# Softmax sums, layernorm centring, weight decoding and instruction order changed in a capped-attention and spatial-gating kernel

## The chip, the cores and the metric

The kernel runs on one core of a Trainium2 chip (trn2). The metric is device time in microseconds of one execution, lower is better. TensorE (PE) multiplies matrices, VectorE (DVE), ScalarE (ACT) and GpSimd (POOL) work on elements, and SyncE (SP) issues almost all DMAs.

## The reference

Capped attention over 4 batches, 12 heads, 448 positions, head width 64, followed by a gated block with a spatial product; all in float32.

```
scores = cap * tanh((q @ k^T / 8) / cap)             # per head
attn   = exp(scores - max) / (sum + 1e-9)
x      = concat over heads of attn @ v                # 4 x 448 x 768
h      = gelu_tanh(x @ w_in)                          # 768 -> 1024
u, v   = h[:, :512], h[:, 512:]
v_n    = (v - mean) / sqrt(var + 1e-6) * g_ln         # over 512
v_s    = w_sg @ v_n + b_sg                            # over positions
out    = x + (u * v_s) @ w_out                        # 512 -> 768
```

## The kernel before, in words

Heads go in pairs, 6 pairs per batch; two pairs make a group, so there are 12 groups, numbered g = 3*batch + group. The 448 keys of a pair are three chunks of 128 and a tail of 64; the tails of a group's two pairs share one step. A step of a group is: scores of a key chunk on TensorE into a PSUM tile `sc` (lines 513 to 547), tanh and exp on ScalarE into a tile `p` of 128 x 896 (591, 593), and the product with the values on TensorE (549 to 568). Most products are made of three float32r matmuls over a high and a low part; the parts are made by a copy and a subtraction (`cop` and `sub`, lines 321 to 326) or, for queries and keys, by a scaling and a fused multiply-subtract (502, 509).

The softmax denominators are sums of `p` over keys. Which engine adds the chunks is chosen for each group in SUMS (line 29). Mode 0: each of the 7 tiles `p` goes to TensorE, which sums over the partitions with a matmul by ones into `den` (line 451). Mode 1: VectorE adds chunks 2 and 3 to chunk 1 for both pairs (line 604, four adds), and the tail tile still goes to TensorE by itself, so 3 units are left. Mode 2: VectorE also adds the halves of the tail tile (two further adds on 64 partitions), and 2 units are left. Two units share a step on TensorE, `den_op`; the last of a batch may be alone.

The denominators are copied out, spread through DRAM, inverted and loaded back (`recip`, 626). Then `gated(b)` (650) runs for each batch: `norm` (666) scales x and splits it, `hv(t)` (719) makes the v half for each block of 128 positions with gelu, statistics, power on GpSimd and layernorm, `hu(f)` (758) the u half, `vsg(f)` (773) the spatial product with bias and gate, `outp(c)` (795) the output product, residual and store. The weights arrive as 64-bit floats and are decoded to a high and a low part by `decode` (359): low, high, shift and sign bits, a whole-number addition on GpSimd (396), then a copy and a subtraction.

Every operation is recorded by `plan.op` (169) with the engines on which it can run and a cost. The order in which they are issued, and the engine of each, is written out by hand: ORDER (37) lists the number of each operation times two, plus one for its second engine. `run` (201) issues them so; each engine then works through its own instructions in that order, and DMAs wait in SP's queue in that order too. Operations wait only for data and for tiles of small pools: 5 `p` tiles (SIZES, 23), 2 `sc` tiles, 3 raw query/key tiles.

Of the kernel before, what the change touches and what calls it, by code (L numbers as in the profile page):

```python
# [28 lines left out]
SUMS = (0, 1, 1, 1, 0, 1, 1, 1, 2, 2, 2, 2)  # L29
PLAIN = (1, 0, 0, 1, 0, 0, 0, 0, 0, 0, 0, 0, 1, 0, 0, 0, 0, 0, 0, 0, 0, 0, 0, 0)  # L30
RETIRE = (10, 10, 12, 11, 0, 0)
# [186 lines left out]
def kernel(  # L218
# [30 lines left out]
    def tiles(n, shape, dtype, name):  # L249
        return [wp.tile(shape, dtype, name=f"{name}{i}") for i in range(n)]  # L250

    win = tiles(2, [128, KD, DFF], FP32R, "win")
    wout = tiles(2, [128, KF, DM], FP32R, "wout")
    wsg = tiles(2, [128, NC, S], FP32R, "wsg")
    LO = NP + 31
# [645 lines left out]
```

## Time and profile before

| | |
|---|---|
| median of 3 runs | 377.01 us (376.59 to 377.73) |
| the profiled execution's own time | 376.92 us |
| its span | 375.1 us |
| busy: PE / PEld / DVE / ACT / POOL | 370.3 / 251.9 / 301.3 / 211.3 / 40.0 us |
| instructions: PE / DVE / ACT / POOL | 2064 / 559 / 275 / 39 |
| DMA | 39.65 MB, 106 GB/s mean |

The span runs from the first to the last instruction or transfer; the execution's own time has 1.8 us around it. PE is the matmul itself, PEld the loading of weights beside it. A group of instructions is named by its line in the kernel and by its tiles, out<-in. A chain of waits is followed back from the last instruction to whatever released it. Instruction durations on VectorE and ScalarE overlap a little: the next one starts some 0.1 us before the one ahead of it has ended, so a sum of durations is more than the time that they fill.

### The profile page before, as it was taken

What the parts mean: (1) busy time and instruction counts of PE and PEld (TensorE: products, weight loads), DVE (VectorE), ACT (ScalarE), POOL (GpSimd) and SP (SyncE); (2) the same over time, 40 slices, a digit from 0 to 9 for tenths busy, and PEclk for the clock granted to TensorE, in tenths of its full rate; (3) what the DMA queues carried; (4) which work ended last, traced back from release to release, by engine and by line L of the source; (5) the groups of instructions that cost most, each with busy time, mean ns of one, the idle gap of its engine ahead of it and who ended that gap; (6) DMA issues with size and microseconds to landing.
All of it is one profiled execution on the core that took longest, in us unless ns stands there. A gap on an engine that the chain in (4) does not pass through costs nothing.

```text
span 375.1 us, 5508 instructions
## 1 busy us (share of the span) xinstructions
PE 370.3 (99%) x2064; PEld 251.9 (67%) x2064; DVE 301.3 (80%) x559; ACT 211.3 (56%) x275; POOL 40.0 (11%) x39
## 2 busy tenths in 40 slices
PE   9999999999999999999999999999999999999995
PEld 4334343455877497546478976486889999889995
DVE  2799999999999999989894779779276988438763
ACT  5999999995685758697914377751031411033200
POOL 0231121510310312030000100000001000001000
PEclk9999999999999999999999999999999999999999
DMA  7898264454371244146520022202120101400004
GB/s 262 290 285 280 91 187 151 118 158 150 98 255 44 65 135 172 43 134 201 150 80 2 20 73 46 76 3 78 36 74 24 47 5 50 171 2 0 2 0 171
DMA packets 23130, 39.65 MB, mean 106 GB/s; under 512 B 5472, under 2 KB 17728, under 8 KB 23104
## 3 DMA queue, kind: packets, MB, share of 16 engines
q1 hardware_dynamic: 22816, 38.96, 33.0%
q8 instruction: 16, 0.26, 0.3%
q10 hardware_dynamic: 288, 0.34, 0.3%
q14 instruction: 10, 0.08, 0.1%
HBM read 33.28 MB, written 6.02 MB: 105 GB/s over the span
## 4 chain that ended last, share of the span: by engine, by line
PE 96%; DVE 2%; ACT 1%; issue 0%; DVEq 0%; ACTq 0%
PE ps L552 15%; PE ps L725 13%; PE ps L763 13%; PE sc L520 11%; PE ps L800 10%; PE ps L780 9%; PE sc L800 6%; PE den L451 5%; PE sc L528 3%; PE sc L763 3%; PE ps L562 3%; PE sc L725 2%; PE sc L536 2%; PE sc L780 1%; PE ps L352 1%; DVE p L604 1%
## 5 line engine op out<-in xcount | busy, mean ns | idle before, releaser
L593 ACT ACTIVATE p<-p,cap 128x896 f32<-128x896 f32 x84 | 84.8, 1041 | 0.7
L591 ACT ACTIVATE p<-sc 128x896 f32<-128x896 f32 x63 | 56.4, 911 | 15.7 <-PE sc L520 6.9
L552 PE MATMUL ps<-p,v 128*64 128x448 f32 x288 | 61.3, 551 | 0.0
L604 DVE TENSOR_TENSOR p<-p,p 128x896 f32<-128x896 f32 (+1 forms) x48 | 53.8, 1130 | 5.5 <-PE ps L552 3.0
L725 PE MATMUL ps<-win,rg 128*128 128x512 f32 x205 | 50.3, 391 | 0.0
L763 PE MATMUL ps<-rg,win 128*128 128x448 f32 x223 | 50.3, 366 | 0.0
L520 PEld LDWEIGHTS sc<-hl 64*128 64x128 f32 x378 | 32.7, 184 | 25.6 <-ACT p L591 11.7
L520 PE MATMUL sc<-hl 64*128 64x448 f32 x378 | 48.3, 383 | 0.0
L763 PEld LDWEIGHTS ps<-rg,win 128*128 128x128 f32 x223 | 41.8, 188 | 4.4 <-issue 0.7
L725 PEld LDWEIGHTS ps<-win,rg 128*128 128x128 f32 x205 | 38.4, 188 | 8.3 <-issue 0.7
L396 POOL TENSOR_TENSOR stage<-stage 128x512 int32<-128x512 int32 (+1 forms) x20 | 30.6, 1532 | 113.4 <-DVE stage L391 58.1
L552 PEld LDWEIGHTS ps<-p,v 128*64 128x64 f32 x288 | 17.5, 136 | 34.1 <-issue 22.0
L706 ACT ACTIVATE t<-ps 128x448 f32<-128x448 f32 (+1 forms) x25 | 14.2, 567 | 46.4 <-PE ps L725 29.3
L800 PE MATMUL ps<-rg,wout 128*128 128x448 f32 x166 | 39.7, 368 | 0.0
L800 PEld LDWEIGHTS ps<-rg,wout 128*128 128x128 f32 x166 | 30.9, 188 | 5.3 <-issue 2.7
L780 PE MATMUL ps<-wsg,rg 128*128 128x448 f32 x130 | 30.6, 369 | 0.0
L711 ACT ACTIVATE t<-t 128x448 f32<-128x448 f32 (+1 forms) x30 | 18.0, 602 | 20.6 <-DVE t L708 20.6
L739 POOL TENSOR_TENSOR sm<-sm,pw 128x1 f32<-128x1 f32 x14 | 8.7, 627 | 186.7 <-DVE sm L737 177.9
L708 DVE SCALAR_TENSOR_TENSOR t<-t,ps 128x448 f32<-128x448 f32 (+1 forms) x25 | 16.2, 647 | 13.3 <-ACT t L706 13.3
L780 PEld LDWEIGHTS ps<-wsg,rg 128*128 128x128 f32 x130 | 24.0, 188 | 4.1 <-issue 1.0
L800 PE MATMUL sc<-rg,wout 128*128 128x448 f32 x98 | 24.3, 365 | 0.0
L591 ACT ACTIVATE p<-sc,qsc 128x896 f32<-128x896 f32 x21 | 21.0, 1005 | 5.4 <-PE sc L536 1.9
(115 smaller groups left out, 468.2 us busy)
## 6 DMA issues: line engine op xcount, KB each, us to landing
raw<-in_qk_dram SPq DMA_DIRECT2D x22, 448.0 KB
stage<-in_w_in_dram SPq DMA_DIRECT2D x12, 512.0 KB
n<-spread SPq DMA_DIRECT2D x24, 224.0 KB
out_dram<-x SPq DMA_DIRECT2D x23, 224.0 KB
v<-in_vp_dram SPq DMA_DIRECT2D x24, 192.0 KB
stage<-in_w_out_dram SPq DMA_DIRECT2D x8, 384.0 KB
u<-in_w_sgT_dram SPq DMA_DIRECT2D x4, 224.0 KB
vt<-in_vt_dram SPq DMA_DIRECT2D x12, 64.0 KB
```

Of the source, the lines that this page charges most:

```text
L396: nc.gpsimd.tensor_tensor(out=a.bitcast(I32), in0=a.bitcast(I32), in1=hi, op=ALU.add)
L451: nc.tensor.matmul(out=den.t[32 * j:32 * j + 32, :S], lhsT=ones_sb[:, kind, NP - 1 - kind - p:NP + 31 - kind - p], rhs=src.t[:, h, :], sta ...
L520: nc.tensor.matmul(out=sc.t[:, h, :S], lhsT=hl[s].t[rows, w, 1, 128 * c - 128:128 * c], rhs=hl[s].t[rows, m, 0], start=(k == 0), stop=(k = ...
L552: nc.tensor.matmul(out=pav[s].t[64 * h:64 * h + 64, :S], lhsT=v[s].t[:, 128 * (c - 1) + 64 * h:128 * (c - 1) + 64 * h + 64], rhs=p.t[:, h, ...
L591: op(name("tanh", s, c), "act", c_act(2 * S, True, raw_scores), lambda p=p, sc=sc, r=raw_scores: nc.scalar.activation(out=p.t, in_=sc.t[:, ...
L593: op(name("exp", s, c), "act", c_act(2 * S, False, True), lambda p=p: nc.scalar.activation(out=p.t, in_=p.t, func=ACTF.Exp, scale=cap_sb), ...
L604: op(name("add", s, t), "dve", c_tt(2 * S), lambda: nc.vector.tensor_tensor(out=a.t[rows], in0=a.t[rows], in1=p.t[rows], op=ALU.add), rd=[ ...
L711: op(tag + " tanh", "act", c_act(n), lambda: nc.scalar.activation(out=view(), in_=view(), func=ACTF.Tanh, scale=GELU_C * GELU_A), wr=[sq])
L725: nc.tensor.matmul(out=ps.t[:, :HF], lhsT=(xl if a else xh)[c].t[:, t * 128:t * 128 + 128], rhs=win[w][:, c, HF:], start=(c == 0 and k == ...
L763: nc.tensor.matmul(out=ps.t[:, :S], lhsT=win[w][:, c, f * 128:(f + 1) * 128], rhs=(xl if a else xh)[c].t[:, :S], start=(c == 0 and k == 0) ...
L780: nc.tensor.matmul(out=ps.t[:, :S], lhsT=(vl if a else vh)[c].t[:, f * 128:(f + 1) * 128], rhs=wsg[w][:, c, :], start=(c == 0 and k == 0), ...
L800: nc.tensor.matmul(out=ps.t[:, :S], lhsT=wout[w][:, f, c * 128:(c + 1) * 128], rhs=(gl if a else gh)[f].t[:, :S], start=(f == 0 and k == 0 ...
```

## The change

SUMS changes for groups 4 to 7, so that VectorE adds more chunks. A mode 3 is written but no group uses it. The "high" step of the decoding can run on ScalarE too. The layernorm is split otherwise: centring, `mean - v`, is one instruction on VectorE or ScalarE that needs only the mean; the multiplication by the inverse deviation goes into the making of the high and low parts, with the deviation as a scalar from a tile; since the sign is turned, the gain `g_ln` is negated once (`gneg`). The statistics tile `sm` is tracked in two parts. Small tiles are allocated between the weight tiles and constants after the pools. Six stores (batch 2, columns 5, and batch 3, columns 0 to 4) are issued as two halves of 112 KB. ORDER is a new table of 1587 entries (1574 before); its text is left out here.

```diff
-SUMS = (0, 1, 1, 1, 0, 1, 1, 1, 2, 2, 2, 2)
+SUMS = (0, 1, 1, 1, 1, 2, 2, 2, 2, 2, 2, 2)
+LANES = (17, 18, 19, 20, 21, 22)
...
-    win = tiles(2, [128, KD, DFF], FP32R, "win")
-    wout = tiles(2, [128, KF, DM], FP32R, "wout")
-    wsg = tiles(2, [128, NC, S], FP32R, "wsg")
+    win = tiles(1, [128, KD, DFF], FP32R, "winh")
+    gneg, cap_sb = small(KF, "gneg"), small(1, "cap")
+    win += tiles(1, [128, KD, DFF], FP32R, "winl")
...
+    op("gneg", "dve", 0.15, lambda: nc.vector.tensor_scalar(
+        out=gneg, in0=g_sb, scalar1=-1.0, scalar2=None, op0=ALU.mult), rd=[k_const], wr=[k_neg])
...
-        def high_bits():
+        def high_bits(e):
             _, hi, a = words()
-            nc.vector.tensor_scalar(out=a, in0=f32(hi), scalar1=2.0 ** -112, scalar2=None, op0=ALU.mult)
+            if e == "dve":
+                nc.vector.tensor_scalar(out=a, in0=f32(hi), scalar1=2.0 ** -112, scalar2=None, op0=ALU.mult)
+            else:
+                nc.scalar.activation(out=a, in_=f32(hi), func=ACTF.Copy, scale=2.0 ** -112)
...
-            op(name("layernorm", t), "dve", 0.55, lambda: nc.vector.tensor_scalar(
-                out=vv(), in0=vv(), scalar1=sm.t[:, 6:7], scalar2=sm.t[:, 0:1],
-                op0=ALU.subtract, op1=ALU.mult), rd=[sm], wr=[v2])
+            def center(e):
+                if e == "dve":
+                    nc.vector.tensor_scalar(
+                        out=vv(), in0=vv(), scalar1=sm.t[:, 6:7], scalar2=-1.0, op0=ALU.subtract, op1=ALU.mult)
+                else:
+                    nc.scalar.activation(out=vv(), in_=vv(), func=ACTF.Identity, scale=-1.0, bias=sm.t[:, 6:7])
+
+            def both(tag, rows, hi, lo, rd, wr_hi, wr_lo):
+                def high(e):
+                    if e == "dve":
+                        nc.vector.tensor_scalar(out=hi(), in0=v2.t[rows, :HF], scalar1=sm.t[rows, 0:1], scalar2=None, op0=ALU.mult)
+                    else:
+                        nc.scalar.activation(out=hi(), in_=v2.t[rows, :HF], func=ACTF.Copy, scale=sm.t[rows, 0:1])
...
+                op("%d v%s lo %d" % (b, *tag), "dve", c_tt(HF) + 0.06, lambda: nc.vector.scalar_tensor_tensor(
+                    out=lo(), in0=v2.t[rows, :HF], scalar=sm.t[rows, 0:1], in1=f32(hi()), op0=ALU.mult, op1=ALU.subtract),
+                   rd=rd + [(sm, "r"), wr_hi], wr=[wr_lo], fast=True)
...
-                cop(name("v hi", t), lambda: h.t, vv, HF, [v2], [h])
-                sub(name("v lo", t), lambda: lo.t, vv, lambda: f32(h.t), HF, [v2, h], [lo])
+                both(("", t), slice(0, 128), lambda: h.t, lambda: lo.t, [v2], (h, 0), (lo, 0))
...
-                out=tt.t[:, :S], in0=ps.t[:, :S], scalar=g_sb[:, f:f + 1], in1=bsg_sb, op0=ALU.mult, op1=ALU.add),
-               rd=[ps, k_const, k_bsg], wr=[tt])
+                out=tt.t[:, :S], in0=ps.t[:, :S], scalar=gneg[:, f:f + 1], in1=bsg_sb, op0=ALU.mult, op1=ALU.add),
+               rd=[ps, k_neg, k_bsg], wr=[tt])
...
+                parts = 2 if not last and b * KD + c in LANES else 1
+                for m in range(parts):
+                    sm = slice(sl.start + cols * m // parts, sl.start + cols * (m + 1) // parts)
+                    op(name("store", c) + "abc"[n + m + (parts > 1)], eng, ISSUE, lambda sl=sm, queue=queue: queue.dma_start(
+                        out=outT[b, c][:, sl], in_=x.t[:, sl]), rd=[(x, sl.start)], size=128 * cols // parts * 4)
```

Read through the codes of both tables, the new one gives TensorE 17 `den_op` steps instead of 21, VectorE 58 adds instead of 48, and ScalarE 9 of the 20 "high" steps, 8 of the 14 centrings and 5 of the 21 scalings of queries and keys, none of which it had; VectorE takes over ScalarE's three denominator copies, the four high copies of the spatial weights, and four x and two g copies, and gives away two evacuations of x, two high copies of `win` and one tail copy.

## Rows read from the trace of the kernel before

**Rows 1.** The page: busy time (share), granted clock in 40 slices, the chain's shares.
```profile
PE 370.3 (99%) x2064; PEld 251.9 (67%) x2064; DVE 301.3 (80%) x559; ACT 211.3 (56%) x275; POOL 40.0 (11%) x39
...
PEclk9999999999999999999999999999999999999999
...
PE 96%; DVE 2%; ACT 1%; issue 0%; DVEq 0%; ACTq 0%
```

**Rows 2.** The chain that ended last, in order: start us, us, what.
```profile
53.45 2.12 DVE p L604
...
63.45 1.64 PE den L451 x16
...
70.37 0.89 PE den L451 x8
...
269.84 5.45 PE ps L725 x24
...
363.32 1.22 PE sc L800 x6
```

**Rows 3.** Stretches: us, busy us of each engine (instructions), clock, DMA, GB/s.
```profile
12.50:50.00 37.50, 37.50 (x262) 14.49 (x262) 35.13 (x58) 36.66 (x42) 8.18 (x5) 1.00 0.65 209
50.00:87.50 37.50, 37.44 (x254) 16.42 (x247) 36.27 (x56) 34.93 (x41) 9.08 (x5) 1.00 0.56 173
87.50:125.00 37.50, 37.50 (x194) 28.00 (x194) 35.80 (x84) 23.95 (x38) 6.44 (x6) 1.00 0.39 120
125.00:162.50 37.50, 37.50 (x230) 23.47 (x228) 35.82 (x68) 28.26 (x38) 8.20 (x7) 1.00 0.38 115
```

**Rows 4.** Line 604, the adds: duration min/median/max, first and last start.
```profile
L604 DVE TENSOR_TENSOR p<-p,p x48: 1076/1084/2209, 26.3 to 255.8; 128x896 f32<-128x896 f32 x40, 64x896 f32<-64x896 f32 x8
```

**Rows 5.** Groups of instructions: xcount | busy us, mean ns | idle before, releasers.
```profile
L593 ACT ACTIVATE p<-p,cap 128x896 f32<-128x896 f32 x84 | 84.8, 1041 | 0.7
...
L591 ACT ACTIVATE p<-sc 128x896 f32<-128x896 f32 x63 | 56.4, 911 | 15.7 <-PE sc L520 6.9 <-DVE p L604 6.6 <-PE ps L552 1.1
L604 DVE TENSOR_TENSOR p<-p,p 128x896 f32<-128x896 f32 (+1 forms) x48 | 53.8, 1130 | 5.5 <-PE ps L552 3.0 <-ACT p L593 1.9
...
L509 DVE SCALAR_TENSOR_TENSOR hl<-raw,root,hl 128x832 fp32r<-128x832 f32 x21 | 22.6, 1077 | 0.1
...
L502 DVE TENSOR_SCALAR hl<-raw,root 128x832 fp32r<-128x832 f32 x21 | 14.4, 686 | 3.2 <-DMA raw<-in_qk_dram 2.3 <-PE sc L520 0.8
...
L382 DVE TENSOR_SCALAR stage<-stage 128x512 f32<-128x512 f32 (+1 forms) x20 | 7.7, 391 | 2.9 <-DMA stage<-in_w_in_dram 2.9
...
L741 DVE TENSOR_SCALAR t<-t,sm 128x512 f32<-128x512 f32 x14 | 7.7, 555 | 2.2 <-POOL sm L739 2.1
...
L297 DVE CAST rg<-u 128x448 fp32r<-128x448 f32 x9 | 3.5, 388 | 0.1
...
L299 ACT ACTIVATE wsg<-u 128x448 fp32r<-128x448 f32 x4 | 2.3, 572 | 0.0
...
L297 DVE COPY t<-den 128x448 f32<-128x448 f32 x1 | 0.6, 623 | 0.3 <-PE den L451 0.3
```

**Rows 6.** In order of time, the start and the end: start us, us, instruction.
```profile
1.17 1.28 ACT L341 ACT_TABLE_LOAD   x1 [1.17 <-PEq L887]
...
6.51 0.65 DVE L502 TENSOR_SCALAR hl<-raw,root 128x832 fp32r<-128x832 f32 x1 [2.33 <-DMA raw<-in_qk_dram]
...
10.26 0.76 DVE L382 TENSOR_SCALAR stage<-stage 128x512 f32<-128x512 f32 x2 [1.64 <-DMA stage<-in_w_in_dram]
...
371.27 0.69 DVE L810 SCALAR_TENSOR_TENSOR x<-sc,x 128x224 f32<-128x224 f32 x2 [0.59 <-PE sc L800]
```

**Rows 7.** In order of time, VectorE, GpSimd and ScalarE: start us, us, instruction.
```profile
53.37 2.19 DVE L604 TENSOR_TENSOR p<-p,p 128x896 f32<-128x896 f32 x1
...
52.93 1.68 POOL L396 TENSOR_TENSOR stage<-stage 128x512 int32<-128x512 int32 x1 [5.73 <-DVE stage L386]
...
55.65 0.92 ACT L591 ACTIVATE p<-sc 128x896 f32<-128x896 f32 x1 [0.66 <-DVE p L604]
```

More of the change, by code (lines that the diff above doesn't have):

```diff
@@ L250, in tiles, with small @@
         return [wp.tile(shape, dtype, name=f"{name}{i}") for i in range(n)]
-    win = tiles(2, [128, KD, DFF], FP32R, "win")
-    wout = tiles(2, [128, KF, DM], FP32R, "wout")
-    wsg = tiles(2, [128, NC, S], FP32R, "wsg")
-    LO = NP + 31
-    const_sb = wp.tile([128, 2 * LO + KF], FP32, name="const_sb")
-    first_sb = wp.tile([128, 129], FP32, name="first_sb")
-    ones_sb = const_sb[:, :2 * LO].rearrange("p (k n) -> p k n", k=2)
-    g_sb = const_sb[:, 2 * LO:2 * LO + KF]
-    cap_in = first_sb[:, 128:]
-    bsg_sb = wp.tile([128, S], FP32, name="bsg_sb")
-    cap_sb = wp.tile([128, 1], FP32, name="cap")
-    qsc = wp.tile([128, 1], FP32, name="qsc")
-    root = wp.tile([128, 1], FP32, name="root")
-    guard = wp.tile([128, 1], FP32, name="guard")
-    pw = wp.tile([128, 1], FP32, name="pw")
+    def small(n, name):
+        return wp.tile([128, n], FP32, name=name)
+    win = tiles(1, [128, KD, DFF], FP32R, "winh")
+    gneg, cap_sb = small(KF, "gneg"), small(1, "cap")
+    win += tiles(1, [128, KD, DFF], FP32R, "winl")
+    qsc, root = small(1, "qsc"), small(1, "root")
+    wout = tiles(1, [128, KF, DM], FP32R, "wouth")
+    guard, pw = small(1, "guard"), small(1, "pw")
+    wout += tiles(1, [128, KF, DM], FP32R, "woutl")
+    sms = tiles(2, [128, 8], FP32, "sma")
+    wsg = tiles(1, [128, NC, S], FP32R, "wsgh")
+    sms += tiles(2, [128, 8], FP32, "smb")
+    wsg += tiles(1, [128, NC, S], FP32R, "wsgl")
+    sm_p = Pool(sms)
+    LO = NP + 31
     stages = [wp.tile([128, 1536], FP32, name=f"stage{i}", tag=f"rg{i}") for i in range(RS // 3)]
@@ L280 @@
     n_p = Pool(tiles(NS, [128, S], FP32, "n"))
-    sm_p = Pool(tiles(4, [128, 8], FP32, "sm"))
+    const_sb = wp.tile([128, 2 * LO + KF], FP32, name="const_sb")
+    first_sb = wp.tile([128, 129], FP32, name="first_sb")
+    ones_sb = const_sb[:, :2 * LO].rearrange("p (k n) -> p k n", k=2)
+    g_sb = const_sb[:, 2 * LO:2 * LO + KF]
+    cap_in = first_sb[:, 128:]
+    bsg_sb = wp.tile([128, S], FP32, name="bsg_sb")
     sc_p = Pool([pp.tile([128, 2, 512], FP32, name=f"sc{i}") for i in range(2)])
@@ L344 @@
         out=guard, in0=guard, scalar1=1e-9, scalar2=None, op0=ALU.mult), wr=[k_guard])
+    k_neg = Buf()
+    op("gneg", "dve", 0.15, lambda: nc.vector.tensor_scalar(
+        out=gneg, in0=g_sb, scalar1=-1.0, scalar2=None, op0=ALU.mult), rd=[k_const], wr=[k_neg])
     def warm():
@@ L399, in decode @@
            rd=[(st, "w")], wr=[(st, "l")], fast=True)
-        op(tag + "high", "dve", c_ts(n), high_bits, rd=[(st, "w"), (st, "h")], wr=[(st, "a")], fast=True)
+        op(tag + "high", BOTH, lambda e: c_copy(e, n) + (0.045 if e == "act" else 0.0), high_bits, rd=[(st, "w"), (st, "h")], wr=[(st, "a")], fast=True)
         op(tag + "shift", "dve", c_ts(n), shift, wr=[(st, "a")], fast=True)
@@ L441, in attention @@
         per = {}
-        total = sum((NU, 3, 2)[s] for s in SUMS[NG * b:NG * b + NG])
+        total = sum((NU, 3, 2, 1)[s] for s in SUMS[NG * b:NG * b + NG])
         def den_op(units):
@@ L618, in group, with fold @@
                     add(per[s], p, c)
+                if SUMS[g] == 3:
+                    if c == FC:
+                        def fold(s=s, src=per[s], dst=per[0]):
+                            nc.vector.tensor_tensor(
+                                out=dst.t[64 * s:64 * s + 64], in0=src.t[:64], in1=src.t[64:], op=ALU.add)
+                        op(name("fold", s), "dve", c_tt(2 * S), fold, rd=[per[s]], wr=[per[0]], fast=True)
+                    if (s, c) == (1, FC):
+                        add(per[0], tail_p, 0)
+                        den_unit(pairs[0], 1, per[0], last)
+                    continue
                 if SUMS[g] == 2 and (c == 0 or (s, c) == (1, 1)):
@@ L734, in hv @@
             sm = Buf(sm_p)
-            op(name("stats", t), "dve", 0.69, lambda: nc.vector.bn_stats(out=sm.t[:, 0:6], in_=vv()), rd=[v2], wr=[sm])
-            op(name("mean", t), "dve", 0.18, lambda: nc.vector.bn_aggr(out=sm.t[:, 6:8], in_=sm.t[:, 0:6]), wr=[sm])
+            op(name("stats", t), "dve", 0.69, lambda: nc.vector.bn_stats(out=sm.t[:, 0:6], in_=vv()), rd=[v2], wr=[(sm, "r")])
+            op(name("mean", t), "dve", 0.18, lambda: nc.vector.bn_aggr(out=sm.t[:, 6:8], in_=sm.t[:, 0:6]),
+               rd=[(sm, "r")], wr=[(sm, "m")])
@@ L737, in hv @@
             op(name("eps", t), "dve", 0.15, lambda: nc.vector.tensor_scalar(
-                out=sm.t[:, 0:1], in0=sm.t[:, 7:8], scalar1=4e-6, scalar2=None, op0=ALU.add), wr=[sm])
+                out=sm.t[:, 0:1], in0=sm.t[:, 7:8], scalar1=4e-6, scalar2=None, op0=ALU.add), rd=[(sm, "m")], wr=[(sm, "r")])
             op(name("power", t), "pool", 0.55, lambda: nc.gpsimd.tensor_tensor(
-                out=sm.t[:, 0:1], in0=sm.t[:, 0:1], in1=pw, op=ALU.pow), rd=[k_pw], wr=[sm], fast=True)
-            op(name("layernorm", t), "dve", 0.55, lambda: nc.vector.tensor_scalar(
-                out=vv(), in0=vv(), scalar1=sm.t[:, 6:7], scalar2=sm.t[:, 0:1],
-                op0=ALU.subtract, op1=ALU.mult), rd=[sm], wr=[v2])
+                out=sm.t[:, 0:1], in0=sm.t[:, 0:1], in1=pw, op=ALU.pow), rd=[k_pw], wr=[(sm, "r")], fast=True)
@@ new lines, in center @@
+            def center(e):
[10 more added lines that the diff above has]
+                        nc.scalar.activation(out=hi(), in_=v2.t[rows, :HF], func=ACTF.Copy, scale=sm.t[rows, 0:1])
+                op("%d v%s hi %d" % (b, *tag), BOTH, lambda e: c_ts(HF) + 0.06 if e == "dve" else c_act(HF, False, True), high,
+                   rd=rd + [(sm, "r")], wr=[wr_hi], fast=True)
+                op("%d v%s lo %d" % (b, *tag), "dve", c_tt(HF) + 0.06, lambda: nc.vector.scalar_tensor_tensor(
+                    out=lo(), in0=v2.t[rows, :HF], scalar=sm.t[rows, 0:1], in1=f32(hi()), op0=ALU.mult, op1=ALU.subtract),
+                   rd=rd + [(sm, "r"), wr_hi], wr=[wr_lo], fast=True)
@@ L744, in hv @@
+            op(name("layernorm", t), BOTH, lambda e: 0.55 if e == "dve" else c_act(HF, False, True), center,
+               rd=[(sm, "m")], wr=[v2], fast=True)
             if t < FC:
                 h, lo = vh[t], vl[t] = Buf(r_p), Buf(r_p)
-                cop(name("v hi", t), lambda: h.t, vv, HF, [v2], [h])
-                sub(name("v lo", t), lambda: lo.t, vv, lambda: f32(h.t), HF, [v2, h], [lo])
+                both(("", t), slice(0, 128), lambda: h.t, lambda: lo.t, [v2], (h, 0), (lo, 0))
@@ L751, in hv @@
                 mine, other = slice(TL * n, TL * n + TL), slice(TL - TL * n, 2 * TL - TL * n)
-                cop(name("v tail hi", n), lambda h=h, m=mine: h.t[m], lambda m=mine: v2.t[m, :HF], HF, [v2], [(h, 0)])
-                sub(name("v tail lo", n), lambda h=h, o=other: h.t[o], lambda m=mine: v2.t[m, :HF],
-                    lambda h=h, m=mine: f32(h.t[m]), HF, [v2, (h, 0)], [(h, 1)])
+                both((" tail", n), mine, lambda h=h, m=mine: h.t[m], lambda h=h, o=other: h.t[o], [v2], (h, 0), (h, 1))
         uu = {}
@@ L812, in outp @@
                    rd=[ps], wr=[(x, sl.start)])
-                op(name("store", c) + "ab"[n], eng, ISSUE, lambda sl=sl, queue=queue: queue.dma_start(
-                    out=outT[b, c][:, sl], in_=x.t[:, sl]), rd=[(x, sl.start)], size=128 * cols * 4)
+                parts = 2 if not last and b * KD + c in LANES else 1
[3 more added lines that the diff above has]
+                        out=outT[b, c][:, sl], in_=x.t[:, sl]), rd=[(x, sl.start)], size=128 * cols // parts * 4)
         if b % 2:
```

158 rows, old and new, of the table ORDER are left out of this document.

## The prediction

> **What bounds the kernel now.** I read the page's busy times first, then the stretches, then the chain. TensorE is busy in 99% of the span, and its granted clock is full (2.4 GHz) throughout [rows 1]. A busy TensorE need not be a full one, so I looked at the spacing: in the chain 24 matmuls of one kind take 5.45 us, and denominator sums that stand apart take 0.89 us each, wherever they stand [rows 2]. The engine streams. The chain that ended last is 96% TensorE [rows 1]. Only around 53 us does it leave TensorE at length: it runs through an add on VectorE that takes 2.12 us [rows 2], for which ScalarE then waits until 55.65 [rows 7].
>
> The Trainium skill, Perfetto Trace Analysis, section "Identifying the Most-Contended Engine", says that matmul occupancy is no measure of TensorE's headroom and that weight-load occupancy should be read instead; by the 67% of that row TensorE would have room. Taken as a verdict on this kernel it would make the work removed below worth nothing, which is the third rival.
>
> The second thing to see is how close the others are. From 12.5 to 87.5 us VectorE stands idle 2.4 + 1.2 us and ScalarE 0.8 + 2.6; from 87.5 to 162.5 VectorE stands idle 1.7 + 1.7 us, ScalarE 13.6 + 9.2 [rows 3]. So the first 88 us are nearly a three-way tie, the next 75 are close between TensorE and VectorE. Over the whole span VectorE is busy for 301 us of 375 [rows 1], so the rest of its 74 idle microseconds lies behind 162 us.
>
> **Part by part.** *Denominators.* The twelve groups go from modes 0,1,1,1,0,1,1,1,2,2,2,2 to 0,1,1,1,1 and then 2. A group costs 7, 3 or 2 sum units, two units share one instruction group, and a batch's last may stand alone: units per batch go from 13,13,8,6 to 13,8,6,6, so TensorE's sum steps from 7+7+4+3 = 21 to 7+4+3+3 = 17. A step costs 0.89 us; two back to back cost 1.64 [rows 2]. The old order joins three pairs, the new one none, so the sum is 15x0.89 + 3x1.64 = 18.3 us before and 17x0.89 = 15.1 after: **-3.2 us of TensorE**. No other matmul is added or removed. The order changes between attention matmuls and full-height ones 27 times instead of 25. Such a change has no row of its own; a sum behind another sum is 0.14 us shorter than one alone, so I take 0.1 each (bounds 0 and 0.14), +0.2: **-3.0 us**.
>
> The price on VectorE: a group that goes from 0 to 1 gains four adds (group 4, batch 1), one that goes from 1 to 2 gains two (groups 5, 6, 7): 10 adds more at a median of 1.08 us [rows 4]. All ten belong to groups whose work lies before 165 us in the old run, the tight stretch.
>
> *What leaves VectorE.* By the new order's codes 9 of 20 "high" decodings (0.39 us each), 8 of 14 centrings (0.555) and 5 of 21 query/key scalings (0.69) go to ScalarE; the four high copies of the gating weights, all three denominator copies that ScalarE had, and a few activation copies come back to VectorE (0.39 to 0.62 each) [rows 5]. Over the whole run: +10.8 for the adds, -3.5, -4.4, -3.4, some +3.5 for the copies, and +1.6 because "v hi" takes its scalar from a tile now (nearest: the old layernorm's 0.555 against a plain copy's 0.39 for 448 columns and some 0.42 for 512, 12 of them): about +4.6 on 301 us. ScalarE, whose centring has no row before, is bounded below by a plain copy of 448 columns (0.572) and above by the exponential of 896 with its scalar from a tile (1.04) [rows 5]; I take 0.72, near the copy since the width is 512. The scalings of 832 columns lie near the exponential, 0.98. With the decodings at some 0.6, by the copy again, ScalarE gets about +12 us on 211, most of it after 87 us, where it has 13.6 us idle in 37.5.
>
> *The new chain of v.* Centring now waits only for the mean and runs beside GpSimd's power; the rest is one scaling and one fused multiply-subtract. The last three VectorE steps become two behind the power, so each tile is ready about 0.4 us sooner; TensorE has other matmuls in between, and I count nothing. The sign is turned once in "gneg" (one tiny instruction) and needs no pass.
>
> *Stores, tiles, start.* Six 224 KB stores become twelve of 112 KB: six more issues on SP, whose loads are all done by then. Nobody waits for them but the end. There the last residuals start at 371.27 and the span ends at 375.1 [rows 6]; the last store is unchanged and was already halved. Bounds: -0.3 (less in flight ahead of it) to +0.6 (an issue and a transfer late); I take 0. Moving small tiles between big ones changes addresses and no instruction: 0, bounds -0.3 to +0.3. At the start SP loads the second and third query/key pairs earlier and values later; TensorE's first steps wait for the same first loads. VectorE's two early waits of 2.33 and 1.64 us for loads [rows 6] may shrink by some 2 us, because the third pair's scaling fills the second one.
>
> *Does VectorE fit?* I take the place where it matters: the last split of the gated product of batch 0 ("0 g lo 3"), which lets TensorE run "0 out 0.3" at 147.9 us in the old run. Read op by op, VectorE has ahead of it, against before: +8 adds (8.6), +8 copies of 0.39 (3.1), one denominator copy (0.6), one fused scaling (1.1), dearer v copies and the sign (0.7): +14.1; and -7 decodings (2.7), -4 centrings (2.2), -2 scalings (1.4), -7 others like the copies here, 0.39 to 0.62 (3.5): -9.8 [rows 5]. Net **+4.3 us**, while TensorE has 3.9 us less ahead of that step (four sums at 0.89 and two output steps of 0.61 less, one value step more, some 0.8 like half a pair of sums) [rows 2]. So 8.2 us must be found on VectorE. Its idle time is about 6.2 us from 12.5 to 147 (the last stretch by its share) [rows 3], plus 4.0 in the first 12 us [rows 6]. Write "found" for how much of this 10.2 us the new order uses. TensorE's remaining work behind that step is 1.0 us more, so the end moves by 4.3 + 1.0 - found, and not below -3.0, where TensorE alone decides. I take found = 7.8, since the 2 us at the start and the short waits of an in-order engine are what another order can fill, and the 5.8 beyond them are rather more than half of the rest: **-2.5 us**. ScalarE is the same story at "1.5 value 3": +0.8 us of work, 2.2 us sooner wanted, 3.4 us idle [rows 3]; it fits with little left.
>
> GpSimd makes some adds dearer: one that began 0.4 us after a GpSimd sum took 2.19 us [rows 7]. The longest add took 2.21, and the mean of all 48 is 1.130 against a median of 1.084 [rows 4, 5]: 2.2 us in all, so two of 48 paid 1.1 each, and ten more adds cost some 0.5, which I count in what is not found. The Trainium skill, Advanced Engine Details and Errata, section "GPSIMD Details", has GpSimd share a read and a write interface with VectorE, in conflict with instructions that read two SBUF inputs, as every add does. The trace agrees as far as that row goes. By that rule every new add that meets GpSimd would pay, and the sum would be the second rival's.
>
> **Sum.** -2.5 us against the profiled execution, 376.92 us (span 375.1, and 1.8 around it), gives 374.4; this execution lies 0.1 under the median of 377.01, so against the median **374.5 us**.
>
> **Rivals.** (1) *VectorE or ScalarE eats most of it.* Found between 4.2 and 6.4 us: the end moves by -1.1 to +1.1, say 377.0. For: ScalarE already waits 6.6 us for adds to free a score tile [rows 5], and the new adds hold tiles longer. Against: the idle time that the sum needs is there. (2) *The adds meet GpSimd, VectorE becomes the bound and it is slower.* Place: the adds of batches 1 and 2 beside the weight decoding; price: five of the ten new adds pay 1.1 us, 5.5 in place of the 0.5 counted, so 2.8 us are found, and 5.3 - 2.8 = +2.5 gives 379.5 us; it decides from found under 4.2 (+1.1 us), some three and a half adds. For: such an add already lies on the chain [rows 2, 7]. Against: two of 48 paid so far, and the order is free to keep them apart. (3) *TensorE is not full.* Removing 3 us of matmuls brings nothing: 377.0. Against it is the even spacing [rows 2]. (4) *The change does not do what it says*: with the centring as another ScalarE function a table could be reloaded; one load took 1.28 us at the start [rows 6], and two for each of eight centrings would put 20 us on ScalarE, of which VectorE would feel a few: 380 or more.
>
> **Chances.** Forecast (found above 6.4): 0.57. Rival 1: 0.20. Rival 2: 0.16. Rival 3: 0.04. Rival 4: 0.03. A measurement of this kernel tells 0.3%, 1.13 us, from no change. Faster is the forecast, 0.57; the same is rival 1 and 3, 0.24; slower 0.19. The range goes from 373.0 (TensorE's full gain of 3.0, the end's 0.3, and the 0.66 us gone for which ScalarE waits for an add at 55.65 [rows 7]) to 378.6, which leaves out most of rival 2 and rival 4; the forecast's own range is 373.0 to 375.9.
>
> **What would show it.** Right: 17 sum steps of 0.89; VectorE's idle from 12.5 to 162.5 us down from 7.0 to 3 or less with TensorE's stream unbroken; the chain still over 90% TensorE; some 58 adds near 1.1 us; one table load. Wrong: gaps in TensorE's stream between 50 and 150 us that end with adds, splits or exponentials; a chain that runs through VectorE for more than 10 us; an end longer than 3.9 us behind the last residual's start.

## The result and the profile after

The changed kernel takes **379.48 us** (median of 6 runs, 378.72 to 380.77) against 377.14 us for the kernel before (6 runs): ratio 1.0067, interval 1.0046 to 1.0088, so 2.3 us slower, where 374.5 and at most 378.6 were forecast. The profiled execution took 379.16 us, with a span of 377.4 (before 376.92 and 375.1).

First the busy times, the clock and the chain from the page of the kernel after, to be read beside [rows 1]; then its stretches up to 200 us, beside [rows 3]:

```profile
PE 370.9 (98%) x2036; PEld 250.6 (66%) x2036; DVE 304.5 (81%) x556; ACT 220.9 (59%) x289; POOL 40.2 (11%) x39
...
PEclk9999999999999999999999999999999999999999
...
PE 77%; DVE 14%; DMA 5%; issue 2%; SPq 1%; POOL 1%; ACT 0%; DVEq 0%
```

```profile
12.50:50.00 37.50, 37.48 (x252) 13.94 (x250) 36.06 (x59) 36.56 (x42) 12.59 (x7) 1.00 0.64 231
50.00:87.50 37.50, 37.27 (x246) 15.27 (x242) 36.35 (x57) 35.65 (x42) 3.03 (x2) 1.00 0.56 165
87.50:125.00 37.50, 37.32 (x186) 28.51 (x184) 36.12 (x85) 25.47 (x42) 8.06 (x8) 1.00 0.29 92
125.00:162.50 37.50, 37.50 (x224) 23.15 (x222) 35.29 (x62) 31.84 (x43) 6.62 (x5) 1.00 0.44 134
162.50:200.00 37.50, 36.39 (x226) 20.49 (x223) 33.42 (x51) 25.80 (x31) 3.73 (x2) 1.00 0.41 123
```

The granted clock is full (1.00 in every stretch shown), so nothing is lost there. VectorE makes up 14% of the chain, 53 us, where it made up 2%: the sign that the prediction named for being wrong. Its idle time from 12.5 to 162.5 us is 1.44 + 1.15 + 1.38 + 2.21 = 6.2 us, not under 3; it was 7.0.

What TensorE lost can be counted from its steps. A step is a group of matmuls that one operation of the program issues; hv, hu, vsg and out are the steps of the functions of these names. I took the time from the start of each step to the start of the next, for its 530 steps before and 526 after; for each pair of kinds that follow each other, the median of the shortest three quarters (both traces together) is what the pair needs, and the rest is counted as waiting. Before: 365.5 us needed, 3.6 waited. After: 362.8 and 8.6. So the work went down by 2.65 us, near the 3.0 forecast, and waits went up by 5.0: 2.7 between 25 and 112 us in pieces of at most 0.36, 1.2 at one place at 184 us, and some 1.2 spread over all 84 hv steps (the 512-column matmuls), whose median went from 0.68 to 0.70 us although no instruction of theirs had changed. That last part is no wait but dearer matmuls, as the runs on placement show.

The groups [rows 4, 5] after, the adds, ScalarE's tanh, and centring on ScalarE (busy us, mean ns, idle before), and then the adds' durations:

```profile
L618 DVE TENSOR_TENSOR p<-p,p 128x896 f32<-128x896 f32 (+1 forms) x58 | 63.7, 1099 | 6.3 <-PE ps L566 4.7
...
L605 ACT ACTIVATE p<-sc 128x896 f32<-128x896 f32 x63 | 56.4, 915 | 11.8 <-DVE p L618 4.2
...
L771 ACT ACTIVATE t<-t,sma 128x512 f32<-128x512 f32 x5 | 3.6, 718 | 2.0 <-DVE sma L760 2.0
```

```profile
L618 DVE TENSOR_TENSOR p<-p,p x58: 1016/1084/1728, 26.9 to 255.6; 128x896 f32<-128x896 f32 x44, 64x896 f32<-64x896 f32 x14
```

58 adds near 1.1 us, as forecast, and none of 2.2 us any more: 58 x (1.099 - 1.084) = 0.9 us above the median in all, against 2.2 before.

### The profile page after: what moved, and what is told of

The parts are those of the page before. It is cut to its first block, busy times and chain, and to the rows that moved or that the text cites. A ratio compares the mean times of both kernels' runs of the same rounds, so it can differ in the third digit from the quotient of the medians.

```text
span 377.4 us, 5488 instructions
## 1 busy us (share of the span) xinstructions
PE 370.9 (98%) x2036; PEld 250.6 (66%) x2036; DVE 304.5 (81%) x556; ACT 220.9 (59%) x289; POOL 40.2 (11%) x39
## 4 chain that ended last, share of the span: by engine, by line
PE 77%; DVE 14%; DMA 5%; issue 2%; SPq 1%; POOL 1%; ACT 0%; DVEq 0%
PE ps L804 12%; PE ps L566 10%; PE ps L749 9%; PE ps L841 9%; PE ps L821 8%; PE sc L534 7%; PE sc L841 5%; DVE p L618 4%; PE sc L804 4%; PE sc L749 3%; PE den L465 3%; PE sc L550 2%; PE ps L576 2%; DVE hl L523 2%; PE sc L821 2%; PE sc L542 2%
## 5 line engine op out<-in xcount | busy, mean ns | idle before, releaser
L749 PE MATMUL ps<-winh,rg 128*128 128x512 f32 x126 | 42.5, 397 | 0.0
L804 PE MATMUL ps<-rg,winh 128*128 128x448 f32 x138 | 39.9, 367 | 0.0
L841 PE MATMUL ps<-rg,wouth 128*128 128x448 f32 x119 | 35.6, 369 | 0.0
L749 PEld LDWEIGHTS ps<-winh,rg 128*128 128x128 f32 x126 | 23.7, 188 | 6.7 <-issue 1.0
L804 PEld LDWEIGHTS ps<-rg,winh 128*128 128x128 f32 x138 | 25.8, 188 | 3.4 <-issue 1.0
L732 DVE SCALAR_TENSOR_TENSOR t<-t,ps 128x448 f32<-128x448 f32 (+1 forms) x23 | 14.9, 647 | 15.6 <-ACT t L730 15.6
L821 PE MATMUL ps<-wsgh,rg 128*128 128x448 f32 x80 | 26.5, 374 | 0.0
L804 PE MATMUL ps<-rg,winl 128*128 128x448 f32 x68 | 24.9, 366 | 0.0
L749 PE MATMUL ps<-winl,rg 128*128 128x512 f32 x62 | 24.6, 397 | 0.0
L841 PEld LDWEIGHTS ps<-rg,wouth 128*128 128x128 f32 x119 | 22.0, 188 | 3.5 <-issue 1.6
L523 DVE SCALAR_TENSOR_TENSOR hl<-raw,root,hl 128x832 fp32r<-128x832 f32 x21 | 23.6, 1125 | 0.1
```

The source lines that it names most:

```text
L523: op(name("qk lo", s), "dve", c_tt(n) + 0.06, lambda: nc.vector.scalar_tensor_tensor(out=used(hl[s].t[:, 1]), in0=used(raw[s].t), scalar=r ...
L749: nc.tensor.matmul(out=ps.t[:, :HF], lhsT=(xl if a else xh)[c].t[:, t * 128:t * 128 + 128], rhs=win[w][:, c, HF:], start=(c == 0 and k == ...
L804: nc.tensor.matmul(out=ps.t[:, :S], lhsT=win[w][:, c, f * 128:(f + 1) * 128], rhs=(xl if a else xh)[c].t[:, :S], start=(c == 0 and k == 0) ...
L821: nc.tensor.matmul(out=ps.t[:, :S], lhsT=(vl if a else vh)[c].t[:, f * 128:(f + 1) * 128], rhs=wsg[w][:, c, :], start=(c == 0 and k == 0), ...
L841: nc.tensor.matmul(out=ps.t[:, :S], lhsT=wout[w][:, f, c * 128:(c + 1) * 128], rhs=(gl if a else gh)[f].t[:, :S], start=(f == 0 and k == 0 ...
```

## Experiments

Medians are given beside those of the kernel before on the same chip. Orders below are the hand-written lists of the two kernels.

**Swapping the sums alone.** The new modes put into the old order, and the old modes into the new one; the order's sums and adds were placed by a simple rule (an add behind the value step that frees its tile, a sum four TensorE steps behind its last input).

```diff
 # kernel before
-SUMS = (0, 1, 1, 1, 0, 1, 1, 1, 2, 2, 2, 2)
+SUMS = (0, 1, 1, 1, 1, 2, 2, 2, 2, 2, 2, 2)
 # kernel after: the reverse
```

> The kernel before with the new modes of groups 4 to 7 alone: 17 sum steps, 58 adds, nothing else moved than these steps and what they force. Theory A (the ten adds make VectorE late between 25 and 112 us and that eats TensorE's 3.2 us): the sums fall by 3.2 us, waits of TensorE rise by 2 to 4 us, 376.0 to 378.5 us. Rival B (the adds are harmless, the rest of the new order is what costs): 374.0 to 375.0 us.

> The changed kernel with the old modes: 21 sum steps, 48 adds, the rest of its order kept. Theory A: TensorE's work rises by 3.2 us and its waits between 25 and 112 us fall from 3.9 to about 1.3, so 379.5 to 380.3 us, near the changed kernel. Rival B: the waits stay, 382 to 383 us.

Measured: 410.89 us (ratio 1.0903) and 400.26 (1.0599), outside both theories. The waits of the first, engine by engine (us in all, times, longest):

```profile
PE sc L507 <- ACT p L578: 10.7, 9, 3.6
PE ps L539 <- ACT p L580: 6.2, 4, 2.9
PE sc L515 <- ACT p L578: 2.9, 4, 1.1
PE ps L712 <- DVE u L700: 2.7, 1, 2.7
```

TensorE waits for the tanh (L578), the exponential (L580) and a gelu's product (L700), and ScalarE for tiles that misplaced adds hold (the same view's row of ScalarE: 25.2 us in 11 waits):

```profile
ACT p L578 <- DVE p L591: 25.2, 11, 4.8
```

These two runs price my rule of placing, not the sums. In the first the granted clock fell as well (0.983 over the whole run, 0.81 from 80 to 90 us, where TensorE was busy for 5.54 us of 10), and that is part of the 34 us. What they suggest is that in this kernel an add in the wrong place costs more than the add; no run moved one add alone. All that follows leaves the two orders as they are, but for one load, and changes sizes, addresses, the way of the layernorm or the engine.

**The late load.** At 184 us TensorE waits 1.11 us for v; in order of time, TensorE's matmul and SP's issues of the kernel after:

```profile
186.10 0.94 PE L566 MATMUL ps<-p,v 128*64 128x448 f32 x3 [1.11 <-DMA v<-in_vp_dram]
```

```profile
177.46 0.58 SPq L324 DMA_DIRECT2D n<-spread  x1
178.15 1.10 SPq L324 DMA_DIRECT2D dsum<-t  x3
179.29 0.36 SPq L857 DMA_DIRECT2D out_dram<-x  x1
179.75 0.38 SPq L324 DMA_DIRECT2D raw<-in_qk_dram  x1
180.17 0.44 SPq L324 DMA_DIRECT2D v<-in_vp_dram  x1
```

v is issued last of a row that stands behind a load of reciprocals (n), which itself waited for a free tile. The experiment moves one entry of the order:

```diff
+    load of v, batch 3, second pair
     load of n, batch 1, fifth row
     ...
-    load of v, batch 3, second pair
```

> The changed kernel with one load moved: the values of pair 1 of batch 3 are issued ahead of the fifth reciprocal row of batch 1, which waits for a free row tile. Theory A with the queue as a second cause: the wait of 1.2 us before the step that uses these values (at 184 us) goes, 378.1 to 378.4 us. Rival: the next late thing (an exponential or a split at the same place) takes its place, 379.2 to 379.6 us.

379.31 us (before 376.97), ratio 1.0057: 0.2 us under the changed kernel, less than the runs scatter, and in the rival's range. The wait at 184 us is gone from its trace (TensorE's waits from 175 to 200 us, counted as above, went from 1.8 to 0.45), but the same run waits 1.6 us at 74.7, in a place where the run shown above waited 0.3. That place comes back below, and the load is tried once more.

**Placement.** The kernel before with the new tile declarations and nothing else:

```diff
-    win = tiles(2, [128, KD, DFF], FP32R, "win")
+    win = tiles(1, [128, KD, DFF], FP32R, "winh")
+    gneg, cap_sb = small(KF, "gneg"), small(1, "cap")
+    win += tiles(1, [128, KD, DFF], FP32R, "winl")
     ...
```

> The kernel before with the new places of the tiles alone (gneg allocated, not used). Theory A: addresses cost nothing, 377.0 to 377.3 us. Rival C (the steps of the v half are 0.70 us in the changed kernel and 0.68 before because the weight tiles moved): +1.0 to +1.2 us, 378.1 to 378.4 us, with 0.70 in its steps.

378.53 us (before 376.97), ratio 1.0035, 1.0024 to 1.0045. So the part that I had bounded at 0.3 us costs 1.56 by itself (1.3 by the ratio). In its chain 24 matmuls of one kind take longer than the 5.45 us of [rows 2]:

```profile
271.32 5.60 PE ps L731 x24
```

**Four parts taken singly.** The change with the old placement; with its ten new adds cut to 32 columns; the kernel before with four sum steps cut; and with the new layernorm.

```diff
 # after_old_place: declarations as before, gneg behind pw
 # after_short_adds, add():
+    w = 32 if g == 4 or g in (5, 6, 7) and t == 0 else S
-    out=a.t[rows], in0=a.t[rows], in1=p.t[rows]
+    out=a.t[rows, :, :w], in0=a.t[rows, :, :w], in1=p.t[rows, :, :w]
 # before_less_sums, den_op(): one matmul of 32 columns where
+    w = 32 if (b, n0) in ((1, 4), (1, 6), (1, 12), (2, 2)) else S
 # before_new_ln: center(), both() and gneg of the change, all on VectorE
```

> The changed kernel with the tiles placed as before the change, nothing else undone. Theory (the placement slows the 512-column matmuls in either order, as placing alone did to the old order, +1.56 us): 377.6 to 378.4 us, the hv steps back from 0.70 to 0.68 us. Rival (in the new order TensorE waits anyway and the dearer steps are hidden in its waits): 379.0 to 379.8, with the steps at 0.68 and the waits longer by as much.

> The changed kernel with each of the ten new adds cut from 2x448 columns to 2x32 (the rest of those denominators' sums is left out), so VectorE is some 9 us lighter and every wait and buffer stays where it is. Theory (the new adds make VectorE late, and TensorE waits for what stands behind them): TensorE's waits from 25 to 112 us, 2.7 us over those of before, go; 376.3 to 377.3 us. Rival (the waits come from the order itself, loads and steps out of place): 379.0 to 379.8.

> The kernel before, with four of its 21 sum steps cut to one matmul of 32 columns (what they add to the denominators is left out) and no add more, so TensorE alone is some 3.0 us lighter. Theory (TensorE bounds the old order, and its sums are worth their time as long as nothing else gets heavier): 373.7 to 374.6 us. Rival (VectorE and ScalarE are already so close behind that TensorE's gain turns into waits): 375.5 to 377.

> The kernel before, with the new way to centre and scale v (and its sign turned once), every step on the engine and in the place that it had. Theory (counted as nothing: two VectorE steps in place of three behind the power, a scalar from a tile dearer by some 0.13 us in 12 of them): 376.5 to 377.5 us. Rival (the fused steps are dearer in the tight first 88 us and make VectorE late): 378 to 379.

Measured, against 377.14: 380.87 (ratio 1.0095), 378.23 (1.0032), 376.69 (0.9985, 0.9972 to 0.9997) and 379.04 (1.0050). The first was outside both theories, the second between its two (1.25 us under the changed kernel), the third in its rival's range, the fourth at the edge of its rival's. The "old placement" was slower than the new one, and the new layernorm cost 1.9 us. What the first and the fourth share is that gneg, a tile of 24 bytes per partition that takes the place of 32, stood ahead of the staging tiles and moved all of those by 32 bytes; and in both, matmuls were dearer to the very end (hv 0.70, out 0.62 us). That became the next theory. The third result is the other half of the story: 2.6 us less for TensorE, and nothing for any other engine to do in return, gained 0.45 us. At two of the four places its trace shows TensorE waiting for ScalarE's tanh at once, as here:

```profile
70.14 0.25 PE L452 MATMUL den<-p,const_sb 128*32 128x32 f32 x2
70.61 0.98 PE L529 MATMUL sc<-raw 64*64 64x448 f32 x8 [0.22 <-ACT p L592]
```

**Addresses.** The same two parts with gneg behind everything else, so that every large tile has its old address; and two kernels in which nothing but one unused tile is added.

```diff
 # before_pad32, before_pad64
+    wp.tile([128, 8], FP32, name="pad")     # 16 for the second
     stages = [wp.tile([128, 1536], FP32, ...
```

> The changed kernel with every large tile at the very address that it had before the change (the six tiny columns of the sign lie behind everything else; in the run with the old placement above they lay ahead of the staging tiles and moved all of those by 32 bytes, as in the run of the new layernorm). Theory (a large tile whose address is not a multiple of 128 bytes makes matmuls that read it dearer, hv 0.68 to 0.70 us, out 0.608 to 0.62): steps back at 0.680 and 0.608, 377.6 to 378.4 us. Rival (addresses only change small things, the waits of the new order set the time): 379.0 to 380.5 us.

> The kernel before with one unused tile of 32 bytes per partition ahead of the staging tiles, so that all tiles behind it start 32 bytes later and no instruction differs. Theory (addresses): 378.6 to 379.2 us, with hv at 0.70 and out at 0.62 us. Rival (addresses do not matter, the new layernorm's steps were what cost 1.9 us in its run): 376.6 to 377.4 us.

> The same with 64 bytes: the weights stay at multiples of 128 bytes, the tiles behind them stand 64 past one. Theory (multiples of 128 are what counts): 377.8 to 378.8 us. Rival (multiples of 64 are enough): 376.6 to 377.4 us.

> The kernel before with the new way to centre and scale v, and now every large tile at its old address. Theory (the steps themselves are worth nothing, the shift by 32 bytes was the 1.9 us): 376.4 to 377.4 us. Rival (the steps make VectorE late in the first 88 us): 378.5 to 379.2 us.

Measured, against 377.27: 378.50 (1.0031, 1.0019 to 1.0043), 379.49 (1.0056, 1.0043 to 1.0069), 377.05 (1.0000) and 376.60 (0.9986, 0.9975 to 0.9996). An unused tile of 32 bytes costs 2.2 us, and no instruction differs. The chains, 24 hv matmuls and 24 out matmuls (start us, us): first with 32 bytes, then with 64.

```profile
270.64 5.60 PE ps L726 x24
...
360.41 4.96 PE ps L801 x24
```

```profile
271.35 5.60 PE ps L726 x24
...
360.00 4.80 PE ps L801 x24
```

The same out matmuls take 4.86 in the kernel before; here is that row of its chain:

```profile
358.46 4.86 PE ps L800 x24
```

With 32 bytes both kinds are dearer, by 3 and by 2%. With 64 the 512-column ones are dearer and the 448-column ones cheaper, and the sum is nothing: neither "multiples of 128" nor "multiples of 64" was the rule. The new layernorm at old addresses is not a cost; it is worth some 0.6 us, hardly clear of the noise (a later run of it with the stores in halves gives 0.9996). And the changed kernel at old addresses gets back some 1.4 us by the ratios (1.0067 to 1.0031) and 1.1 by the medians, in two sets of runs, and is still slower than before.

**What eats TensorE's saving.** Four more, of which the last asks whether VectorE's load can move:

```diff
 # less_sums_less_adds: e7's cut, and in add():
+    w = 32 if g in (1, 2, 3, 5) and t == 3 else S
 # after_al_short: old addresses and the ten adds cut as above
 # after_al_vload: old addresses and the load of v moved as above
 # new_ln_act: new layernorm at old addresses, centring of batch 0 and of batch 1's
 #             first two tiles on ScalarE, in the same places of the order
```

> The kernel before with four sum steps cut, as in the run that gained only 0.45 us, and eight of its old adds (the second of each pair's in groups 1, 2, 3 and 5) cut to 2x32 columns as well, some 8 us less on VectorE; what these add to the denominators is left out. Theory (VectorE was what TensorE's saving ran into): most of the 2.6 us of TensorE's sums is gained now, 374.0 to 375.3 us. Rival (ScalarE, or loads, are the next bound): 376.2 to 377.0.

> The changed kernel with every large tile at its old address and the ten new adds cut to 2x32 columns (the rest of those sums is left out). Theory (the adds on VectorE are what keeps the aligned one above before): 376.0 to 377.2 us, 1.3 to 2.5 under the aligned one. Rival (order and ScalarE): 378.0 to 378.6.

> The changed kernel with every large tile at its old address and the load of v of the last batch's second pair issued ahead of the batch 1 reciprocals' load that it stood behind on SP. Theory (TensorE's wait at 184 us is on the path): its 0.6 to 1.2 us go, 377.3 to 377.9 us. Rival (what is gained there is lost on VectorE behind it): 378.3 to 378.7.

> The kernel before with the new way to centre and scale v, large tiles at their old addresses, and six centrings (batch 0's four, batch 1's first two) on ScalarE in the same places of the order. Theory (VectorE bounds the stretch to 165 us, ScalarE has room there): 375.6 to 376.4 us, 0.2 to 1.0 under the one with all centrings on VectorE. Rival (VectorE's lateness is spent ahead of 87 us, or ScalarE's centring makes v late): 376.5 to 377.5.

Measured, against 377.17: 376.01 (0.9963, 0.9948 to 0.9978), 377.43 (1.0002, 0.9989 to 1.0016), 377.75 (1.0024, 1.0006 to 1.0042), 376.59 (0.9989, 0.9978 to 1.0000). The first falls between its theories: with 8 us taken off VectorE's adds (6.0 off its busy time, 301.3 to 295.3), 1.2 us of 2.6 are gained. Its trace says what came next. In order of time, TensorE and VectorE; L691 multiplies a tail of x by the reciprocals, L715 makes the gelu's last product and empties a PSUM tile:

```profile
108.92 0.47 PE L765 MATMUL ps<-r,win 128*128 128x448 f32 x1 [1.14 <-DVE u L715]
```

```profile
107.35 0.23 DVE L691 TENSOR_TENSOR n<-x,n 128x64 f32<-128x64 f32 x1 [0.72 <-DMA n<-spread]
107.75 0.20 DVE L297 CAST r<-n 128x64 fp32r<-128x64 f32 x1 [0.17 <-DVE n L691]
107.97 0.23 DVE L325 TENSOR_TENSOR rg<-n,r 128x64 fp32r<-128x64 f32 x1
108.12 0.22 DVE L691 TENSOR_TENSOR n<-x,n 128x64 f32<-128x64 f32 x1
108.25 0.61 DVE L715 SCALAR_TENSOR_TENSOR u<-t,ps 128x448 f32<-128x448 f32 x1
```

TensorE needs the PSUM tile that L715 empties; L715 stands in VectorE's queue behind L691, which now arrives before its load of reciprocals does. In the kernel before, VectorE's same step (L689 there) started 0.9 us later and without a wait:

```profile
108.28 0.19 DVE L689 TENSOR_TENSOR n<-x,n 128x64 f32<-128x64 f32 x1
```

So behind TensorE stands VectorE, and close behind VectorE stand the loads. The second run prices the ten adds at 1.1 us of time (378.50 to 377.43) for 8.6 us of VectorE's work (305.3 us busy to 296.7). The traces show a place where they cost it. In the changed kernel at old addresses a sum step waits for the last of group 4's new adds and is broken in two, 2.5 us in place of 0.89. TensorE and VectorE:

```profile
73.56 0.95 PE L460 MATMUL den<-p,const_sb 128*32 128x448 f32 x4
75.18 0.95 PE L460 MATMUL den<-p,const_sb 128*32 128x448 f32 x4 [0.67 <-DVE p L613]
```

```profile
74.04 1.08 DVE L613 TENSOR_TENSOR p<-p,p 128x896 f32<-128x896 f32 x1
```

With the adds cut, the same step is whole:

```profile
74.78 0.96 PE L460 MATMUL den<-p,const_sb 128*32 128x448 f32 x8
```

It is the place where the run with the late load moved waited 1.6 us and the profiled run of the kernel after only 0.3, so what is lost there differs from run to run. The third of the four prices the late load at 0.75 us by the medians and 0.3 by the ratios, with runs from 376.67 to 380.10 and intervals that overlap the one without it, so that stays open. The fourth gains nothing over centring on VectorE (376.60).

**Stores, and a better placement.** The new layernorm at old addresses with the six stores in halves; and without halves, with the staging tiles 64 bytes further and the first weight's two tiles as well.

```diff
 # new_ln_both64
+    cap_sb, qsc (32 bytes each) ahead of win; root, guard between win and wout
+    two of the four sm tiles ahead of the staging tiles
```

> The kernel before with the new way to centre and scale v, large tiles at their old addresses, and the six stores in halves. Theory (the stores are off the path): as without the halves, 376.2 to 377.0 us. Rival (six more issues and transfers in SP's queue hold up something): 377.2 to 378.

> The kernel before with the new way to centre and scale v; the staging tiles and all behind them 64 bytes further (as in the run with a 64 byte tile, where hv steps went up to 0.70 us and hu, out and vsg down to 0.60), and now the two tiles of the first weight 64 bytes further as well, the other weights at multiples of 128. Theory (what counts for a matmul is how its two operands stand to each other): hv back at 0.68, out and vsg at 0.60, hu at 0.608, 375.0 to 376.2 us. Rival (each operand's own address counts): hv at 0.70 or more, 376.5 to 377.5 us.

Measured, against 376.99: 376.93 (0.9996, 0.9985 to 1.0006), not to be told from 0.9986 without halves; and **375.71** (0.9973, 0.9961 to 0.9986), 1.3 us under the kernel before and the fastest of all. How much of that is the placement and how much the new layernorm is not settled: the interval of the new layernorm alone, 0.9975 to 0.9996, overlaps. Its chain's shares, and its hv and out rows:

```profile
PE 98%; ACT 0%; DVE 0%; DVEq 0%; issue 0%
```

```profile
268.85 5.48 PE ps L732 x24
...
357.29 4.85 PE ps L824 x24
```

With win moved along, hv is back at 5.48 (5.60 when only the tiles that it meets had moved); vsg stayed at 0.600 us a step, out was at 0.607. For hv, then, what counts in these runs is how its two operands stand to each other. For out that is not shown: 0.60 had been expected of it, as with the 64-byte tile, and it came out near the 0.608 of before.

## Why the prediction was wrong

**The work taken from TensorE** was right: 17 sum steps of 0.889 us, 2.65 us less instead of 3.0.

**"0, bounds -0.3 to +0.3" for the tiles failed**, on the reasoning "changes addresses and no instruction". By themselves the declarations cost 1.56 us, and undone in the changed kernel 1.1 to 1.4. The trace of before could not show this, and a range for it should have come from a row: over 300 steps of hv, hu, vsg and out at some 0.6 us each are some 200 us of TensorE, of which 1% is 2 us.

**"I take found = 7.8" failed.** Of the 10.2 idle microseconds VectorE used 7.0 - 6.2 = 0.8 from 12.5 to 162.5 us, and by its busy time in the first 12.5 us (5.43 against 4.77) 0.7 more. By the prediction's formula 1.5 found would give +3.8 us. The measured excess at old addresses is 1.2, so the sum of late work was too strict while the room was far too generous: cutting the ten adds, of which the formula counts eight at 8.6 us ahead of its place, gave 1.1. The idle time could not be filled because most of it is waiting for something that does not come earlier. In the new order two such waits are new, in the stretch where VectorE has 2.6 us idle in all: 1.2 us for GpSimd ahead of a copy of win, and 0.88 us here. In order of time, VectorE's copy of batch 0's denominators and what it does with their return, after:

```profile
51.28 0.61 DVE L304 COPY t<-den 128x448 f32<-128x448 f32 x1
...
59.01 0.38 DVE L661 SCALAR_TENSOR_TENSOR d<-d,guard 64x84 f32<-64x84 f32 x1 [0.88 <-DMA d<-dsum]
...
70.18 0.63 DVE L695 TENSOR_TENSOR x<-x,n 128x448 f32<-128x448 f32 x1
```

and before, the copy's row of the tile den (first and last start 47.6) and the same two steps:

```profile
L297 DVE COPY t<-den x1: 623/623/623, 47.6 to 47.6; 128x448 f32<-128x448 f32 x1
```

```profile
63.19 0.29 DVE L637 SCALAR_TENSOR_TENSOR d<-d,guard 64x84 f32<-64x84 f32 x1
...
72.46 0.62 DVE L671 TENSOR_TENSOR x<-x,n 128x448 f32<-128x448 f32 x1
```

The copy stands 3.7 us later and the result is wanted 4.2 us sooner, so the way out and back through DRAM has 7.7 us where it had 15.6. The way is on the chain of the kernel after, and so is a split of queries and keys ahead of the copy (L523, median 1.08 us) that met a GpSimd instruction:

```profile
48.65 2.04 DVE hl L523
...
51.36 0.54 DVE t L304
...
52.99 1.38 DMA dsum<-t
...
54.43 4.56 DMA d<-dsum
...
59.01 0.38 DVE d L661
```

No run moved this copy by itself: that it is part of the 1.2 us left at old addresses is argued from three traces of the new order (it waits 0.88, 0.52 and 0.75 us in them), not shown.

**That TensorE decides** was the assumption under both. The chain of 96% [rows 1] is true, and misled: it says that every wait of TensorE's is short, not that its work is all that matters. Four sums less gained 0.45 of 2.6 us. The third rival gave the right answer to this run (removing matmuls brings next to nothing), though not for its reason. It was built on the Trainium skill, Perfetto Trace Analysis, section "Identifying the Most-Contended Engine", which judges TensorE's room by MFU (the share of its peak rate that the matmuls use) and by its weight loads, not by its matmuls' busy share. This case's trace does not bear that out: with weight loads at 67%, TensorE's steps needed 365.5 of the 375.1 us at their own spacing. What ate the saving was that ScalarE, VectorE and the loads were as late as TensorE was.

**The new chain of v**, counted as nothing, gains some 0.6 us: centring on VectorE takes 0.48 us for 0.555 and no longer waits for the power (2.1 us before, of which 1.4 reappear ahead of "v hi" in the kernel after). On ScalarE it takes 0.718 us; 0.72 had been taken. **The stores** are still 0 as far as the runs can tell; the span ends 3.8 us behind the last residuals' start, 3.9 before. Rival 4 did not come: ScalarE's function table is still loaded once.

**The rivals.** The first (VectorE and ScalarE eat most) had the mechanism; with the placement's 1.4 us added its 377.0 would be 378.4. The second named 379.5 and the measured time is 379.48, by accident: the adds paid less for GpSimd than before (0.9 us in all). The Trainium skill, Advanced Engine Details and Errata, section "GPSIMD Details", has an instruction with two SBUF inputs in conflict with GpSimd. The trace does not bear out a price for each add that meets it: of the 58 adds seven overlap a GpSimd instruction; the four that began before it paid nothing, the three that began during it 0.04, 0.32 and 0.65 us. Nor is it the adds alone that pay: the VectorE instructions that took over 0.15 us more than the median of their kind, all of them beside a GpSimd instruction, are twelve with 8.1 us in all before and nine with 6.5 after. So meeting GpSimd is not what made the kernel slower, though the split of 2.1 us on the chain above is one such meeting.

**Sum, by ratios** (1.0067 is +2.5 us): addresses +1.4, new layernorm -0.5, ten adds +1.1, four sums -0.6. That leaves some 1.1 us for the order itself, with the late v and the denominators' way perhaps among it; no run shows what it is made of. These were priced in different settings and need not add up.

## What to carry to other kernels

A chain that is nearly all one engine does not mean that taking work from that engine is worth its time: cut the work crudely, leave the rest, and see what is gained, before paying for it on another engine. Idle time of an in-order engine is room only where what ended it can come earlier too; read what ends it. When a tile is added or moved, look at the addresses of all that lies behind it, and time that by itself.

## What was not expected of the hardware

Matmul time depends on where the operands lie in SBUF, with every instruction the same. No trace shows an address: those below are counted from the sizes of the tiles declared ahead, each rounded up to 32 bytes, from the start of the pool. For 24 hv matmuls (512 columns moving): 5.45 us with both operands at multiples of 128 bytes, 5.60 with the stationary one 32 or 64 bytes past, 5.48 with both 64 past. For 24 out matmuls (448 columns moving): 4.86 with both at multiples of 128, 4.96 with the moving one 32 past, 4.80 to 4.85 with it 64 past. VectorE and ScalarE took as long as they had (busy for 301.3 and 211.5 us with the 32-byte tile, 301.3 and 211.3 without). Why is open; only these and the mixed one of the change were tried.
